# First batch loaded in four transfers on two queues, its second softmax placed later, second column pair whole, a new written order

## The chip, the cores and the metric

The kernel runs on one core of one Trainium2 chip. The metric is the device time of one execution in microseconds (us). The core has a matrix engine (PE, with a weight load PEld that runs beside it), a vector engine (DVE), a scalar engine (ACT), a general engine (POOL), and SyncE (SP), which here only issues transfers. Each engine runs its own instructions in the order in which they are written and waits for the others through semaphores. Transfers (DMAs) are issued by SP, ACT and POOL.

## The reference

Two stages. The first lets `x` [8, 8, 512, 64] (batch, head, row, feature) and `state` [8, 8, 32, 64] read each other by two softmaxes; the second is a two-layer network with a PReLU between, over the 544 rows of each batch, 4352 rows of 512 in all.

```python
a  = softmax(x @ state.T / 8)          # over the 32 states:  xread = a @ state   (512 rows)
a2 = softmax(state @ x.T / 8)          # over the 512 rows:   sread = a2 @ x      (32 rows)
rows = concat([xread, sread])          # heads side by side: 512 columns
h = rows @ w_in                        # 512 -> 2048
g = max(h, 0) + alpha * min(h, 0)      # alpha per column
out = g @ w_out                        # 2048 -> 512
```

All inputs and the output are float32.

## The kernel before

Everything is in float16 for PE, with sums in float32. The `xread` rows are never formed: per batch the kernel makes `m = state @ w_in` (step "m", its copy "mo"), and then `h = m.T @ a.T` directly. A batch has 16 column parts of 128 columns of `h` ("F", two 512-column matmuls each). Batch 0 can also be worked in pieces: "f" does a pair of column parts for one half of the rows (four 256-column matmuls), with "n" and "g" for its PReLU. The PReLU of a whole part is "N" on ACT (`neg = relu(-h)`) and "G" on DVE (`g = h + (1 - alpha) * neg`). The second layer of batch 0 is plain ("S" matmuls, "O" copies out). Batches 1 to 7, and a batch 8 which is the 256 `sread` rows, use seven products in place of eight ("P"), with sums of weights "W" and of activations "U" on POOL, kept copies "K" and quarters of the output "Q".

The attention steps of one batch are these. "lx" loads `x` (POOL's queue, cast to float16 on the way); "xd" transposes it by a DMA issued by SP into `xT`; for batch 0 PE transposes it ("xt", copies "xo"), since it is needed at once, and batch 1's is done likewise. "sc" are the scores. From them come two softmaxes:

- over the states: "sb" (a transpose on DVE), "smax", "ssh", "sexp" (ACT), "ssum", "snorm" and "wb" (a transpose on DVE), which gives `aT`, the moving operand of the column parts. For batch 0 the scores are computed a second time with the rows on the partitions ("tsc", from `st_pairs`, filled by "sbd"), in two halves, and `aT` comes by PE ("at", copies "ao").
- over the rows, for the state reads: "tm" (a maximum on DVE), "nb" (its scaling), "te" (two exponentials on ACT), "tsum", "tn", "tt" (a transpose by a DMA issued by SP into `e2T`), and then "rd" (32 small matmuls) with its copy "rdo" into `XS`. `XS` is wanted only by batch 8's column parts, near the end.

Before any of this "stc", "stt" and "sto" bring batch 0's states into `stT`, and "str" and "sro" the states of the other batches, in two groups (0: batches 1 and on, 1: the later ones), from the load "lst". "wi.0" to "wi.3" load `w_in` by 512 columns, "wo.0" to "wo.3" `w_out` by 512 rows, all on POOL's queue. "oma" makes `1 - alpha`.

What sets the order of the work is one string, `ORDER` (L18): a list of such steps, written out by hand, with their batch, part and PSUM bank or engine as arguments. The program runs through it and issues every step's instructions to the engines in that order; no scheduler moves them. `F.1.5.3` is batch 1, column part 5, PSUM bank 3; a letter behind a step is its engine (a: ACT, v: DVE, p: POOL). `Z.k.n` are n fill matmuls into bank k, whose result nobody reads; before the list starts there are 16 more of them. There are six single PSUM banks (k0 to k5) and one double ("two"), each with one buffer: a step that writes to a bank waits until the last reader of what stood there is done. So an early or late PReLU shows up as a wait of a matmul for its bank. Copies of the output go through four `osb` buffers (L643 and on, and L741 and on), each freed by the landing of the transfer that SP issues from it.

Ahead of the list stand, in this order: the load of batch 0's `x`, 512 KB per half `j` of the rows, both on SP (`load_x0`, L162); the load of batch 0's states on ACT's queue; a memset on DVE and four small loads of `alpha` on SP; the fill pattern and the identity on POOL; and the memset of `st_pairs` on DVE.

## Time and profile before

| | us |
|---|---|
| median of 3 runs | 213.96 (213.93 to 214.35) |
| the profiled execution | 214.07 |
| its span, first to last instruction | 212.0 |
| PE busy | 203.3 (96%), 2034 matmuls |
| DVE busy | 174.2 (82%) |
| ACT busy | 152.6 (72%) |
| POOL busy | 179.1 (84%) |
| granted TensorE clock, mean | 1.00 |

Times in the profile count from the first instruction of the span. Busy is the time in which an engine has work under way, also when that work stalls: matmuls are pipelined and their ends are modelled, so 96% says that PE is nearly always the engine at work, not that it runs at its peak. The chain of waits is followed back from the last instruction to whatever released each step. DVE's share is an average: near 100% over the middle of the span, and less towards the end, where no attention is left to do.

### The profile page before, as it was taken

Reading aid. Unit: us, or ns where it says so; the run is one execution under the profiler, and the core shown is the slowest. Engines: PE = TensorE matmul, PEld = TensorE weight load, DVE = VectorE, ACT = ScalarE, POOL = GpSimd, SP = SyncE. Lnnn points to the kernel's source line nnn. Section 1 sums busy time; section 2 is a strip of 40 time slices with the busy share of each in tenths; the row PEclk is TensorE's granted clock in tenths of the full one; section 3 lists DMA queues with packets and bytes.
Section 4 is the critical chain, followed back from the end, with each engine's and each line's share of the span. In section 5 each row is a group of like instructions: output and inputs, shape, how many; then the busy total and the mean of one; then the engine's idle time right before and its main releaser. Section 6 shows DMA issues by size and latency. Waiting matters only on the chain.

```text
span 212.0 us, 5108 instructions
## 1 busy us (share of the span) xinstructions
PE 203.3 (96%) x2034; PEld 137.7 (65%) x2034; DVE 174.2 (82%) x260; ACT 152.6 (72%) x300; POOL 179.1 (84%) x111
## 2 busy tenths in 40 slices
PE   7899999999999999999999998999999999999991
PEld 4556333444666665677667875667688777888880
DVE  0787988999999999999999999898999777654340
ACT  2577979999999999999797777887954584234100
POOL 8048848998999899999996999479996999999860
PEclk9999999999999999999999999999999999999999
DMA  6999995966665436778744539011521201111232
GB/s 159 219 204 207 206 204 89 160 165 90 152 105 89 106 84 135 110 134 143 183 117 49 103 106 192 3 51 40 162 53 49 99 3 49 49 53 49 74 124 102
DMA packets 43975, 23.70 MB, mean 112 GB/s; under 512 B 22192, under 2 KB 43440, under 8 KB 43952
## 3 DMA queue, kind: packets, MB, share of 16 engines
q1 hardware_dynamic: 31904, 15.22, 27.9%
q0 software_dynamic: 11776, 8.09, 26.6%
q8 instruction: 16, 0.26, 0.5%
q10 hardware_dynamic: 272, 0.07, 0.1%
q14 instruction: 7, 0.06, 0.1%
HBM read 17.31 MB, written 8.91 MB: 124 GB/s over the span
## 4 chain that ended last, share of the span: by engine, by line
PE 88%; DMA 7%; ACT 2%; issue 1%; SPq 0%; DVE 0%; ACTq 0%
PE h L556 25%; PE px L715 23%; PE pv L715 12%; PE o L626 6%; PE py L715 5%; PE m_ps L507 4%; PE h L565 3%; PE fill L236 3%; DMA xT<-xg 2%; DMA x<-in_x_dram 2%; PE sr_ps L480 2%; DMA out_dram<-oq 2%; DMA e2T<-e 1%; PE sc L314 1%; PE xT_ps L299 1%; PE h L578 1%
## 5 line engine op out<-in xcount | busy, mean ns | idle before, releaser
L612 DVE SCALAR_TENSOR_TENSOR g<-neg,oma_sb,h 128x512 f16<-128x512 f32 (+1 forms) x140 | 92.7, 708 | 11.6 <-ACT neg L609 11.1
L609 ACT ACTIVATE neg<-h 128x512 f32<-128x512 f32 (+1 forms) x140 | 75.0, 585 | 23.0 <-PE h L556 14.4
L556 PE MATMUL h<-aT,m 128*128 128x512 f16 x248 | 67.2, 379 | 0.1
L715 PEld LDWEIGHTS <-gsum 128*128 128x128 f16 x480 | 46.1, 98 | 16.8 <-issue 1.8
L715 PEld LDWEIGHTS <-g 128*128 128x128 f16 x360 | 35.0, 98 | 9.1 <-issue 0.9
L694 POOL TENSOR_TENSOR gsum<-g 128x1024 f16<-128x1024 f16 (+1 forms) x16 | 32.0, 2009 | 4.2 <-DVE g L612 3.6
L694 POOL TENSOR_TENSOR gsum<-g,g 128x1024 f16<-128x1024 f16 (+1 forms) x16 | 32.0, 2004 | 3.9 <-DVE g L612 3.8
L556 PEld LDWEIGHTS <-m 128*128 128x128 f16 x248 | 23.7, 98 | 15.5 <-issue 0.8
L694 POOL TENSOR_TENSOR gsum<-gsum,g 128x1024 f16<-128x1024 f16 (+1 forms) x16 | 32.1, 2006 | 1.1
L715 PE MATMUL px<-ws,gsum 128*128 128x256 f16 x240 | 32.6, 273 | 0.0
L694 POOL TENSOR_TENSOR gsum<-g,gsum 128x1024 f16<-128x1024 f16 (+1 forms) x16 | 31.9, 2005 | 0.1
L731 ACT COPY kept<-px 128x512 f32<-128x512 f32 (+1 forms) x22 | 12.7, 577 | 14.0 <-PE px L715 13.7
L533 ACT CAST m<-m_ps 128x512 f16<-128x512 f32 x36 | 20.0, 613 | 1.8 <-PE m_ps L507 1.5
L384 POOL TENSOR_TENSOR ts<-ts,mx 128x1024 f32<-128x1024 f32 x7 | 13.4, 1908 | 5.4 <-DVE mx L379 5.4
L715 PE MATMUL px<-w_out_sb,gsum 128*128 128x256 f16 x120 | 17.4, 273 | 0.0
L715 PE MATMUL pv<-ws,gsum 128*128 128x256 f16 x120 | 17.2, 273 | 0.0
L748 DVE TENSOR_TENSOR oq<-pv,kept 128x512 f32<-128x512 f32 (+1 forms) x16 | 10.5, 655 | 8.1 <-PE pv L715 6.7
L626 PE MATMUL o<-w_out_sb,g 128*128 128x512 f16 x64 | 17.1, 380 | 0.0
L715 PE MATMUL pv<-ws,g 128*128 128x256 f16 x120 | 16.9, 273 | 0.0
L715 PE MATMUL px<-w_out_sb,g 128*128 128x256 f16 x120 | 16.9, 273 | 0.0
L715 PE MATMUL py<-w_out_sb,g 128*128 128x256 f16 x120 | 16.2, 273 | 0.0
L531 ACT CAST m<-m_ps 128x1024 f16<-128x1024 f32 x12 | 12.4, 1032 | 1.3 <-PE m_ps L507 1.2
(76 smaller groups left out, 251.6 us busy)
## 6 DMA issues: line engine op xcount, KB each, us to landing
out_dram<-oq SPq DMA_DIRECT2D x28, 256.0 KB, 2.5
xg<-in_x_dram POOLq DMA_DIRECT2D x7, 512.0 KB, 6.9
w_in_sb<-in_moe_w_in_dram POOLq DMA_DIRECT2D x4, 512.0 KB, 9.3
...
```

The costliest lines, as they stand in the source:

```text
L384: engine(e).tensor_tensor(blocks(cols(live["ts", b], j, S)), blocks(scored(b, j)), over_blocks(cols(live["mx", b], j, S // N)), ALU.subtract,)
L507: nc.tensor.matmul(t[N * k : N * (k + 1), :], st_head(b, h)[64 * r : 64 * r + 64, :], w_in_sb[64 * r : 64 * r + 64, c, 512 * f : 512 * (f ...
L531: copier(e)(m_tile(b, f), t)
L533: copier(e)(m_tile(b, f)[:, g, :], t[g])
L556: nc.tensor.matmul(h.rearrange("p (r j s) -> p r j s", r=2, j=2), ms[b, f][:, g, 128 * j : 128 * (j + 1)], weights(b, g), start=(g == 0), ...
L609: nc.scalar.activation(neg, h, RELU, bias=0.0, scale=-1.0)
L612: nc.vector.scalar_tensor_tensor(g_tile(b, jc), negs.pop((b, jc)), oma_sb[:, jc : jc + 1], hs.pop((b, jc)), ALU.mult, ALU.add,)
L626: nc.tensor.matmul(outs[b, q], g_tile(b, jc)[:, 128 * q : 128 * (q + 1)], w_out_sb[:, jc, :], start=not begun and jc == 2 * jc2, stop=left ...
L694: engine(e).tensor_tensor(t, x(), y(), op)
L715: nc.tensor.matmul(pbanks[b, name][:, i, :], of(b, c)[:, j, 128 * i : 128 * (i + 1)], moving[:, 4 * c + j, :], start=not begun and j == 0, ...
L731: copier(e)(t, pbanks[b, "x"])
L748: nc.vector.tensor_tensor(osb, pbanks[b, name], kept[b, add], ALU.add)
```

## The change

It rewrites `ORDER` as a whole (1117 steps before, 1109 after; the same matmuls do the needed work, in another order) and edits the code around it:

- Batch 0's `x` comes in four loads of 256 KB (four heads each) in place of two of 512 KB. The first half of the rows is issued by SP, the second by ACT, behind the load of batch 0's states.
- `alpha`'s memset and loads become a step, "la", which stands behind the first loads of the weights; the two memsets go from DVE to POOL.
- The load of the other batches' states is split: "lst.0" stands behind "wi.0", "lst.1" far later, and "str.1" and "sro.1" with it.
- In the list, batch 0's second softmax (the scores "sc.0", then "tm.0", "nb.0", "te.0") stands behind batch 1's scores "sc.1" and the maxima and exponentials "te" made of them, in place of between the halves of the first softmax. Batch 1's scores come earlier.
- The second pair of column parts of batch 0 (parts 2 and 3) is done whole (`F.0.2`, `F.0.3`) in place of in two row halves (`f.0.1.0`, `f.0.1.1`).
- The casts of the second half of `x` are on ACT, that of batch 0's states on DVE.
- The loads of the weights go in another order: before `wi.0 lst lx.1 wi.1 wo.0 wo.1 wi.2 wi.3 wo.2 wo.3`, after `wi.0 lst.0 lx.1 wi.1 wi.2 wo.0 wo.1 wi.3 wo.2 wo.3`, with the two norms "snorm.p.0" between `wo.0` and `wo.1`.
- In batch 5, "tt.5" and "rd.5" stood next to each other but for one step "m"; now the column parts and products of batches 2 to 4 between them come to some 6 us of PE. At the end of the list the last copies out have new engines and places (`K.8.2` on ACT), and three fills stand last.
- The other steps have new places within their stage, and new banks. The fills of the list are 42 both before and after, in 16 groups before and 8 after.

The list's start and end, and the code:

```diff
-Z.0.3 stc.a stt.0 cx.0.1.v xt.0.0.1.1 xo.0.0.1.a wi.0 cx.0.0.v xt.0.0.0.2 xo.0.0.0.a sbd.0.v lst sbd.1.v Z.3.2 sto.a
-Z.3.2 Z.3.3 cx.1.0.v xt.0.1.0.3 cx.1.1.v tsc.0.1.4 tsc.0.0 smax.0.0 ssh.v.0.0 xo.0.1.0.a xt.0.1.1.5 xo.0.1.1.a Z.1.3
-Z.1.2 sc.0.0 sc.0.1 tsc.1.1.1 m.0.0.2.0 tsc.1.0 sexp.0.0 tm.0 smax.0.1 ssum.0.0 Z.3.3 mo.0.0.a.1 lx.1 Z.3.2 Z.3.2
-Z.3.3 ssh.v.0.1 str.1.3 nb.0.a te.0.1 Z.5.3 str.0.5 Z.4.3 Z.4.3 te.0.0 sexp.0.1 Z.4.2 mo.0.0.v.0 Z.4.3 wi.1 ssum.0.1
-wo.0 sro.0.a xt.1.0.0.4 snorm.p.0.0 at.0.0 ao.0.a wo.1 Z.1.3 tsum.0 snorm.p.0.1 xt.1.0.1.1 m.1.0 xt.1.1.0.2 sro.1.a
-wi.2 oma.a xo.1.0.0.v wi.3 xo.1.0.1.v xo.1.1.0.a f.0.0.0.5 xt.1.1.1.0 n.0.0.0 mo.1.0.v at.1.4 ao.1.v m.0.1.1.3
-tn.0.1.p mo.0.1.v.1 m.1.1 mo.1.1.a g.0.0.0.0 g.0.0.0.1 f.0.0.1.2 n.0.0.1 f.0.1.1.4 mo.0.1.a.0 n.0.1.1 f.0.1.0.3
-xo.1.1.1.v g.0.0.1.1 g.0.0.1.0 sc.1 tm.1 m.2.0.5.0 mo.2.0.a.1 mo.2.0.a.0 F.0.5.1 N.0.5 F.0.4.2 N.0.4 nb.1.a te.1.1
-g.0.1.1.0 g.0.1.1.1 G.0.5 S.0.3.0.0 wo.2 G.0.4 S.0.1.0.5 S.0.1.1 sb.1 F.0.7.4 N.0.7 G.0.7 F.0.6.1 wo.3 tn.0.0.p N.0.6
-S.0.3.1 G.0.6 n.0.1.0 g.0.1.0.0 S.0.2.2.2 S.0.3.2 te.1.0 S.0.1.2 S.0.2.0 g.0.1.0.1 m.0.2 S.0.2.3 S.0.1.3 smax.1
-mo.0.2.a F.0.8.4 N.0.8 G.0.8 W.1.1.p F.0.11.1 N.0.11 G.0.11 tsum.1 F.0.10.3 N.0.10 m.0.3 mo.0.3.a W.1.0.p lx.2 S.0.2.1
-S.0.3.3 F.0.9.4 m.1.2 F.0.12.1 ssh.p.1 sexp.1 G.0.10 S.0.2.5 S.0.1.5 ssum.1.s N.0.9 G.0.9 F.0.13.3 S.0.3.5 mo.1.2.a
-m.1.3 N.0.12 G.0.12 S.0.3.4 F.0.15.4 tn.1.1.a N.0.13 G.0.13 F.0.14.1 S.0.1.4 S.0.3.6 S.0.1.6 W.2.0.p S.0.2.4 N.0.15
...
-F.5.1.5 N.5.1 G.5.1 P.4.5.0.1 P.4.5.0.0 F.5.6.3 N.5.6 P.4.5.1.1 G.5.6 P.4.5.1.0 tt.5 m.7.1.1.2 rd.5.4 mo.7.1.a.0 sc.7
-rdo.5.a m.6.3.5.1 mo.6.3.a.0 U.4.3.0.p F.5.0.3 P.4.7.0.0.4 mo.7.1.a.1 tm.7 mo.6.3.a.1 F.5.13.5 P.4.7.1.0 N.5.13 N.5.0
...
-U.7.4.0.p N.8.0 G.8.0 F.8.10.5 U.8.3.1.p P.7.5.1.0 K.7.4.a P.8.2.0.1.2 N.8.10 G.8.10 P.7.7.1.0 P.8.1.0.0.4 U.8.3.0.p
-P.7.2.1.0.3 Q.7.1.1 P.7.2.0.1 P.7.2.0.0 P.7.3.0.1 P.7.2.1.1 U.8.1.0.p P.7.3.1.0 P.7.4.0.1 P.8.1.0.1 P.7.3.0.0 Q.7.0.0
-K.8.1.a P.7.4.1.1 U.8.2.0.p P.8.6.0.0 P.7.4.0.0 P.7.4.1.0 Q.7.1.0 U.8.1.1.p U.8.2.1.p P.8.6.0.1 K.8.2.v P.7.3.1.1
-P.8.7.0.0.5 P.8.5.0.1 P.8.5.0.0 K.8.4.a P.8.7.0.1 P.8.2.0.0 U.8.4.0.p Q.7.0.1.v P.8.3.0.0 Q.8.1.1 P.8.4.0.1 U.8.4.1.p
-P.8.4.0.0 Q.8.0.0 Q.8.1.0 P.8.3.0.1 Q.8.0.1.a
+cx.0.0.v xt.0.0.0.0 stc.v cx.0.1.v cx.1.0.a cx.1.1.a stt.1 xo.0.0.0.v xt.0.0.1.2 Z.3.3 sbd.0.v sbd.1.v tsc.0.0.3
+xo.0.0.1.v tsc.0.1 smax.0.0 xt.0.1.0.4 xo.0.1.0.v xt.0.1.1.5 sto.a wi.0 lst.0 xo.0.1.1.a Z.0.6 ssh.v.0.0 sexp.0.0 lx.1
+tsc.1.0.0 tsc.1.1 Z.2.6 smax.0.1 ssh.v.0.1 wi.1 ssum.0.0 m.0.0.2.1 mo.0.0.a.0 sexp.0.1 str.0.4 Z.5.9 ssum.0.1 Z.5.3
+sro.0.a wi.2 wo.0 m.1.0 mo.1.0.v la m.2.0.5.3 xt.1.1.0.0 xt.1.1.1.2 xo.1.1.1.v mo.0.0.a.1 xt.1.0.1.4 mo.2.0.a.0
+xo.1.1.0.a snorm.p.0.0 at.0.1 xo.1.0.1.a xt.1.0.0.5 xo.1.0.0.v ao.0.v snorm.p.0.1 at.1.0 ao.1.a Z.2.3 oma.a sc.1
+mo.2.0.a.1 f.0.0.1.2 sb.1 wo.1 F.0.2.4 n.0.0.1 N.0.2 m.0.1.5.1 wi.3 wo.2 Z.0.9 F.0.3.0 mo.0.1.a.1 mo.0.1.a.0 F.0.5.3
+tm.1 wo.3 g.0.0.1.1 smax.1 g.0.0.1.0 nb.1.a te.1.1 te.1.0 G.0.2 N.0.3 G.0.3 F.0.4.1 F.0.6.5 N.0.6 G.0.6 N.0.5 tsum.1
+G.0.5 m.0.2 mo.0.2.a f.0.0.0.2 F.0.7.4 N.0.7 G.0.7 N.0.4 G.0.4 S.0.1.0.0 n.0.0.0 ssh.p.1 lx.2 xd.2 S.0.1.1 g.0.0.0.0
+S.0.3.0.5 g.0.0.0.1 S.0.3.1 m.1.1 F.0.11.3 F.0.10.4 sexp.1 S.0.3.3 mo.1.1.a ssum.1.s W.1.0.p S.0.0.1.1 F.0.8.2 N.0.11
+S.0.1.3 G.0.11 N.0.10 G.0.10 N.0.8 G.0.8 S.0.3.2 S.0.0.0 m.0.3 mo.0.3.a F.0.9.3 N.0.9 S.0.0.3 S.0.1.2 sc.0.0 sc.0.1
+G.0.9 tm.0 F.0.12.4 N.0.12 F.0.13.2 F.0.14.3 G.0.12 N.0.13 S.0.3.5 nb.0.a te.0.0 W.1.1.p snorm.p.1 wb.1 G.0.13 W.2.0.p
+te.0.1 W.2.1.p S.0.1.4 tn.1.0.p S.0.0.5 F.0.15.4 N.0.15 G.0.15 tsum.0 N.0.14 G.0.14 S.0.1.5 m.1.3 S.0.3.4 F.1.2.2
+S.0.1.6 mo.1.3.a N.1.2 G.1.2 tn.0.1.p tn.1.1.p tn.0.0.p W.3.0.p F.1.7.4 N.1.7 G.1.7 F.1.5.3 N.1.5 S.0.1.7 O.0.1.a tt.0
+S.0.0.4 F.1.13.2 N.1.13 F.1.3.4 G.1.5 G.1.13 N.1.3 G.1.3 F.1.12.0 N.1.12 tt.1 G.1.12 F.1.14.3 N.1.14 G.1.14 m.1.2
+mo.1.2.a F.1.6.2 N.1.6 S.0.0.7 F.1.0.4 N.1.0 S.0.0.6 m.2.2.0.3 mo.2.2.a.1 mo.2.2.a.0 sc.2 G.1.6 lst.1 S.0.0.2 O.0.0.a
+tm.2 nb.2.a sb.2 smax.2 F.1.15.2 F.1.4.3 N.1.15 G.1.0 S.0.2.7.0 F.1.8.1 S.0.3.7 N.1.4 G.1.4 S.0.2.3 S.0.3.6 S.0.2.1
+W.3.1.p te.2.0 te.2.1 tsum.2 G.1.15 O.0.3.a F.1.1.4 N.1.1 N.1.8 m.3.2 rd.0.5 rdo.0.a rd.1.3 G.1.8 W.4.0.p str.1.2
+S.0.2.4 G.1.1 S.0.2.6 ssh.p.2 sexp.2 lx.3 S.0.2.2 S.0.2.5 rdo.1.a ssum.2.5 S.0.2.0 U.1.1.1.p mo.3.2.a sro.1.a
+U.1.3.0.p tn.2.1.p snorm.v.2 m.2.3.1.4 mo.2.3.a.0 m.2.1 O.0.2.v F.1.9.3 N.1.9 F.1.11.2 P.1.1.0.1.1 P.1.1.0.0 P.1.1.1.0
+N.1.11 mo.2.3.a.1 mo.2.1.a wb.2 F.1.10.5 G.1.9 F.2.8.0 F.2.11.4 N.1.10 U.1.2.1.p F.2.2.3 G.1.11 G.1.10 N.2.11 xd.3
...
+F.4.13.5 N.4.13 xd.6 P.2.3.1.0 Q.2.0.1.a U.3.1.1.p tn.5.0.a G.4.13 tn.5.1.a tt.5 U.3.2.1.p F.4.15.0 N.4.15 sb.5
+F.4.11.3 N.4.11 G.4.15 P.3.1.0.1.1 P.3.1.1.0 P.3.1.1.1 P.3.1.0.0 P.2.4.1.0 F.4.14.4 K.3.1.a Q.2.1.0 N.4.14 F.4.12.5
+F.4.1.0 P.3.6.1.0 G.4.11 N.4.1 G.4.14 G.4.1 P.3.6.0.0 N.4.12 G.4.12 F.4.10.2 N.4.10 G.4.10 sc.6 rd.5.3 rdo.5.a rd.4.4
...
+U.7.3.1.p K.8.1.a U.7.4.0.p U.7.4.1.p U.8.1.1.p P.7.7.0.1 P.7.7.1.1 P.7.3.0.1 P.7.3.1.1 Q.7.1.1 P.7.3.1.0 P.7.4.1.0
+P.7.4.1.1 P.7.4.0.1 U.8.1.0.p U.8.2.0.p P.7.4.0.0 Q.7.1.0 U.8.2.1.p P.8.6.0.1 P.8.6.0.0 K.8.2.a P.7.3.0.0 U.8.3.0.p
+P.8.7.0.0.5 Q.7.0.1.v P.8.5.0.1 P.8.5.0.0 K.8.4.a U.8.3.1.p P.8.7.0.1 P.8.2.0.1.4 U.8.4.0.p Q.8.1.1 U.8.4.1.p
+P.8.2.0.0 P.8.4.0.1 P.8.4.0.0 Q.8.0.0 Q.8.1.0 P.8.3.0.0 P.8.3.0.1 Q.8.0.1.a Z.1.3
...
 """
 
 
@@ -146,6 +145,8 @@
         return ps.tile(shape, dtype, name=name, tag="two", bufs=1)
 
     def copier(e):
+        if e == "p":
+            return nc.gpsimd.tensor_copy
         return nc.scalar.copy if e == "a" else nc.vector.tensor_copy
 
     def engine(e):
@@ -167,29 +168,35 @@
         xgs[0] = att.tile([128, H, 2, 2, D], F16, name="xg_0", tag="xg", bufs=3)
         for j in range(2):
             t = att.tile([128, H, 2, D], F32, name=f"x0_{j}", tag="ts", bufs=2)
-            nc.sync.dma_start(
-                t, x[0, :, 256 * j : 256 * (j + 1), :].rearrange("k (p r) d -> p k r d", r=2)
-            )
+            for g in range(2):
+                heads = slice(4 * g, 4 * g + 4)
+                (nc.scalar if j else nc.sync).dma_start(
+                    t[:, heads, :, :],
+                    x[0, heads, 256 * j : 256 * (j + 1), :].rearrange("k (p r) d -> p k r d", r=2),
+                )
             x0s.append(t)
 
     def x0_cast(j, g, e):
         copier(e)(xgs[0][:, 4 * g : 4 * g + 4, j, :, :], x0s[j][:, 4 * g : 4 * g + 4, :, :])
 
-    load_x0()
     rows = state.rearrange("b h n d -> (b h n) d")
     n0 = H * N
     n_j = (B * H * N - n0) // 128
     w_st = n_j // 2
     st0_32 = consts.tile([128, 2, D], F32)
     nc.scalar.dma_start(st0_32, rows[:n0, :].rearrange("(g p) d -> p g d", p=128))
+    load_x0()
     alpha_rows = consts.tile([128, N], F32)
-    nc.vector.memset(alpha_rows, 0.0)
-    for q in range(4):
-        nc.sync.dma_start(
-            alpha_rows[N * q : N * q + n_jc, :],
-            moe_alpha.rearrange("(jc q p) -> q jc p", q=4, p=N)[q],
-        )
     alpha_sb = consts.tile([128, N], F32)
+
+    def load_alpha():
+        nc.gpsimd.memset(alpha_rows, 0.0)
+        for q in range(4):
+            nc.sync.dma_start(
+                alpha_rows[N * q : N * q + n_jc, :],
+                moe_alpha.rearrange("(jc q p) -> q jc p", q=4, p=N)[q],
+            )
+
     pattern = consts.tile([128, 256], F16)
     nc.gpsimd.iota(
         pattern, pattern=[[37, 256]], base=-4800, channel_multiplier=29,
@@ -199,10 +206,10 @@
     make_identity(nc, ident)
     st = consts.tile([128, n_j, D], F16)
 
-    def load_states():
+    def load_states(i):
         nc.gpsimd.dma_start(
-            st.rearrange("p (i j) d -> p i j d", i=2),
-            rows[n0:, :].rearrange("(i p j) d -> p i j d", i=2, j=w_st),
+            st[:, w_st * i : w_st * (i + 1), :],
+            rows[n0:, :].rearrange("(i p j) d -> i p j d", i=2, j=w_st)[i],
         )
 
     w_in_sb = consts.tile([128, n_c, d_ff], F16)
@@ -227,7 +234,7 @@
     XS = consts.tile([128, n_c, 2, N, B // 2], F16)
 
     st_pairs = consts.tile([128, H, 2, N], F16)
-    nc.vector.memset(st_pairs, 0.0)
+    nc.gpsimd.memset(st_pairs, 0.0)
 
     def fill(k, n):
         t = single(k, f"fill_{len(zs)}", [128, 256], F32)
@@ -374,9 +381,9 @@
             return cols(live["ts", b], j, S)
         return live["tsc", j].rearrange("p r h n -> p (r h n)")
 
-    def state_max(b, j=None):
+    def state_max(b, j=None, e="v"):
         soft_tiles(b)
-        nc.vector.tensor_reduce(
+        engine(e).tensor_reduce(
             cols(live["mx", b], j, S // N), blocks(scored(b, j)), AX.X, ALU.max
         )
 
@@ -392,14 +399,14 @@
         ts = cols(live["ts", b], j, S)
         nc.scalar.activation(ts, ts, EXP, bias=0.0, scale=scale)
 
-    def state_sum(b, jk):
+    def state_sum(b, jk, e="v"):
         j = None if b else jk
         if jk == "s":
             live["r1", b] = att.tile([128, 2 * S // N], F32, name=f"r1_{b}", tag="r1", bufs=2)
         elif b:
             live["r1", b] = single(jk, f"r1_{b}", [128, 2 * S // N], F32)
         r1 = cols(live["r1", b], j, S // N)
-        nc.vector.tensor_reduce(r1, blocks(cols(live["ts", b], j, S)), AX.X, ALU.add)
+        engine(e).tensor_reduce(r1, blocks(cols(live["ts", b], j, S)), AX.X, ALU.add)
         nc.vector.reciprocal(r1, r1)
 
     def state_norm(e, b, j=None):
@@ -752,11 +759,11 @@
     steps = {
         "lst": load_states, "wi": load_w_in, "wo": load_w_out, "lx": load_x,
         "stc": first_states_cast, "stt": first_states_transposed, "sto": first_states_out,
-        "oma": one_less_alpha, "sbd": first_states_paired, "str": states_transposed, "sro": states_out,
+        "la": load_alpha, "oma": one_less_alpha, "sbd": first_states_paired, "str": states_transposed, "sro": states_out,
         "xd": x_transposed_dma, "xt": x_transposed, "xo": x_out, "sc": scores, "cx": x0_cast, "tsc": token_scores,
         "at": tokens_transposed, "ao": tokens_out,
         "sb": score_blocks, "smax": state_max, "ssh": state_shift, "sexp": state_exp,
-        "ssum": state_sum, "snorm": state_norm, "wb": weights_back,
+        "ssum": state_sum, "smx": lambda e, b: state_max(b, None, e), "ssm": lambda e, b: state_sum(b, "s", e), "snorm": state_norm, "wb": weights_back,
         "tm": token_max, "nb": token_shift, "te": token_exp, "tsum": token_sum, "tn": token_norm,
         "tt": token_transposed, "rd": state_reads, "rdo": state_reads_out,
         "m": state_w_in, "mo": state_w_in_out,
```

More of the change, by code (lines that the diff above doesn't have):

```diff
@@ new lines @@
+N.6.2 G.6.2 F.6.14.2 P.5.1.1.1.3 P.5.1.0.1 N.6.14 G.6.14 F.6.3.5 P.5.1.1.0 N.6.3 G.6.3 F.6.8.4 m.7.1.1.0 U.5.1.1.p
+rd.6.2 N.6.8 rdo.6.v mo.7.1.a.0 rd.7.5 U.5.1.0.p U.5.2.0.p rdo.7.a mo.7.1.a.1 F.6.15.1 F.6.6.2 N.6.6 P.5.2.0.0.5
+smax.7 P.5.1.0.0 U.5.2.1.p K.5.1.a F.6.11.0 N.6.11 N.6.15 G.6.8 G.6.6 G.6.11 G.6.15 F.6.4.4 F.6.1.2 P.5.6.0.0
+P.5.2.1.1 P.5.6.1.1 F.8.9.0 N.6.4 G.6.4 N.8.9 G.8.9 F.6.12.1 N.6.12 G.6.12 ssh.p.7 F.6.10.4 N.6.1 G.6.1 P.5.6.1.0
+P.5.6.0.1 K.5.2.a N.6.10 G.6.10 sexp.7 P.5.2.1.0 F.8.13.0 ssum.7.1 snorm.v.7 P.5.2.0.1 P.5.5.0.1 Q.5.0.0 U.5.3.1.p
```

107 lines of the change are left out of this document (47 added, 60 removed).

## The prediction

> **What bounds the kernel now.** I read the page's first part, then the groups by shape, then the chain, then the waits and the timeline of the first 40 us. The page (busy shares; the chain's shares):
>
> ```profile
> PE 203.3 (96%) x2034; PEld 137.7 (65%) x2034; DVE 174.2 (82%) x260; ACT 152.6 (72%) x300; POOL 179.1 (84%) x111
> ...
> PE 88%; DMA 7%; ACT 2%; issue 1%; SPq 0%; DVE 0%; ACTq 0%
> ```
>
> Groups of PE by shape (count; busy us, mean ns), then the chain that ended last (start, us, what) and PE's waits:
>
> ```profile
> L556 PE MATMUL h<-aT,m 128*128 128x512 f16 x248 | 67.2, 379 | 0.1
> ...
> L715 PEld LDWEIGHTS <-gsum 128*128 128x128 f16 x480 | 46.1, 98 | 16.8 <-issue 1.8 <-POOL gsum L694 0.4
> L715 PEld LDWEIGHTS <-g 128*128 128x128 f16 x360 | 35.0, 98 | 9.1 <-issue 0.9
> ...
> L626 PE MATMUL o<-w_out_sb,g 128*128 128x512 f16 x64 | 17.1, 380 | 0.0
> ...
> L236 PE MATMUL fill<-pattern 128*128 128x256 f16 x58 | 10.5, 306 | 1.8 <-POOL pattern L194 1.2
> ```
>
> ```profile
> 51.47 1.11 ACT neg L609 x2
> ...
> 62.55 1.31 PE px L715 x12
> 63.86 1.73 PE h L556 x8
> ...
> 129.30 2.85 DMA e2T<-e
> 132.29 0.68 PE sr_ps L480 x32
> ...
> 204.43 3.57 DMA out_dram<-oq
> 208.00 0.02 issue
> ...
> 208.18 0.37 ACT oq L746
> ```
>
> ```profile
> PE sr_ps L480 <- DMA e2T<-e: 1.0, 1, 1.0
> PE xT_ps L299 <- DVE xg L176: 0.5, 1, 0.5
> PE sc L314 <- DMA xT<-xg: 0.4, 1, 0.4
> ```
>
> The chain is PE. Back to back, a 256-column matmul takes 1.31/12 = 0.109 us and a 512-column one 1.73/8 = 0.216 us. So the needed stream is 840 x 0.109 + (248 + 64) x 0.216 = 159 us, and some 30 us of smaller groups (m, transposes, scores, reads, batch 8): 188.7 us, the same before and after. The span is this, plus what PE loses, plus the end. I count loss as start of an instruction minus the needed work ordered ahead of it. The 58 fills are loss too. Where it arises is read from the timeline of the start:
>
> ```profile
> 7.18 0.76 DVE L176 CAST xg<-x 128x512 f16<-128x512 f32 x2 [0.36 <-DMA x<-in_x_dram]
> ...
> 9.41 0.69 DVE L384 TENSOR_TENSOR ts<-tsc,mx 128x512 f32<-128x512 f32 x1
> ...
> 10.09 1.23 DVE L426 TENSOR_REDUCE nb<-sc 128x2 f32<-128x1024 f32 x1
> ...
> 10.14 0.63 ACT L393 ACTIVATE ts<-ts 128x512 f32<-128x512 f32 x1 [0.61 <-DVE ts L384]
> ...
> 11.59 0.69 ACT L443 ACTIVATE e<-sc,nb 128x512 f16<-128x512 f32 x1
> ...
> 12.26 0.68 ACT L443 ACTIVATE e<-sc,nb 128x512 f16<-128x512 f32 x1
> ...
> 14.03 0.69 DVE L402 TENSOR_REDUCE r<-ts 128x16 f32<-128x512 f32 x1
> ...
> 14.75 0.25 DVE L403 RECIPROCAL r<-r 128x16 f32<-128x16 f32 x1
> ...
> 15.16 1.04 POOL L406 TENSOR_TENSOR an<-ts,r 128x512 f16<-128x512 f32 x1 [0.41 <-ACT stT L282]
> ...
> 17.36 0.91 ACT L282 COPY stT<-st_ps 128x896 f16<-128x896 f16 x1
> ...
> 18.12 0.60 PE L578 MATMUL h<-aT,m 128*128 128x256 f16 x4
> ...
> 18.32 0.58 ACT L304 COPY xT<-xT_ps 128x512 f16<-128x512 f16 x1
> ...
> 22.09 4.22 POOL L670 TENSOR_TENSOR ws<-w_out_sb 128x1024 f16<-128x1024 f16 x2 [1.44 <-DMA w_out_sb<-in_moe_w_out_dram]
> ...
> 24.04 1.40 DVE L612 SCALAR_TENSOR_TENSOR g<-neg,oma_sb,h 128x512 f16<-128x512 f32 x2
> ...
> 38.23 0.59 PE L556 MATMUL h<-aT,m 128*128 128x512 f16 x2
> ```
>
> Ahead of the first column part (18.12) stand 4.2 us of needed work: 13.9 lost. Ahead of batch 1's first column (38.23) stand 22.6: 15.6 lost. So nearly all loss is the start. Later come 3.0 us: about 1.0 to 1.1 in the read of batch 5's e2T at 132.29, about 0.5 in batch 3's scores, 1.3 in small steps between m matmuls and other banks. PE ends at 207.5, but the last copy starts at 208.18, behind an output's landing (204.43 + 3.57): it reuses that output's buffer.
>
> **The change, part by part.**
>
> First x. The same 1 MB and the 64 KB of states move, in four loads on two queues instead of two on one. Today the second half of x lets its cast start at 7.18. No row shows x on ACT's queue. Bounds: the rate of today with the last part 1 us later (8.2), or the second half as early as the first half is now, whose cast starts 7.18 - 0.36 less the 0.88 us of casts, 5.9 at the most. I take 7.0, nearest to today's row. The casts of that half move to ACT (0.57 each, by the 0.58 of its copies).
>
> The Trainium skill, "DMA: Bandwidth & Descriptors", section "Issuing engines are not separate DMA queues", says that loads issued from several engines run on the same 16 DMA engines, and that only issue time is saved. By that rule the landing stays near 7.2 and the sum loses 0.2 us.
>
> Batch 0's softmax. Today DVE's maximum for the reads (1.23 at 10.09) and ACT's two exponentials (0.67 apart) sit between the two halves of the other softmax. They, the scores and the nb step go behind. What follows, by rows: last cast done 7.6; transposes and copy to 8.7; second scores 9.4; maximum 0.69 to 10.1; shift 0.69 to 10.8; m.0.0 and its copy go ahead on ACT (0.5), exponential 0.63 to 11.9; sum and reciprocal 0.69 + 0.25 to 12.9; POOL's norm 1.04 to 14.05. Today that norm ends at 16.2. Then ACT is the bound: state copy (to 12.7), two m copies, two xT copies, aT copy, each 0.5 apart, to 16.0. Scores of batch 1 go at 16.0, the first part at 16.4 with 4.5 us of work ahead: 11.9 lost against 13.9.
>
> The gain is partly given back. Batch 1's softmax now comes before batch 0's columns: transpose, two maxima (some 1.2 each, as the row at 10.09) on DVE, two exponentials on ACT, while PE runs nine fills of Z.0.9 (1.4 us with the change of bank) and then waits for the scores' bank (exponential done 20.75, m.0.2 at 20.9) and for G.0.3 (22.25). From there each G takes 1.40 - 0.74 = 0.66 us from start to start and each N 1.11 - 0.61 = 0.50, and I place them one by one behind their matmuls and banks: S.0.1.0 at 22.4 with 8.5 us ahead (13.9 lost), F.0.8 at 26.2 with 12.3 (13.9), F.0.15 at 32.7 with 18.6 (14.1), F.1.5 at 35.8 with 21.5 (14.3). Today 15.6. **Start: -1.3 us**, -0.3 to -2.0.
>
> Loads on POOL's queue. They land one behind the other; issue to landing:
>
> ```profile
> L212 POOL DMA_DIRECT2D w_in_sb<-in_moe_w_in_dram x4: 747/792/972, 1.6 to 17.0; - x4
> ...
> DMA to landing us min/median/max: 7.8/9.3/12.7
> ```
>
> The third part of w_in now stands ahead of the first of w_out, and half the states go later (lst.1). First w_out: POOL's row at 22.09 shows the second one landing at 22.1, and a load takes some 2.5 us, so the first lands at 19.5 today; 2.5 later, less 0.6 for the states and 0.2, it lands at 21.2, and its first use is at 22.4. The others have 1 to 3 us of cover. If that cover is gone, each us late is a us lost. lst.1 issues at about 39 and is read by PE at about 48: free. The alpha loads move behind the w_in loads, are used at 15.8, and are free; POOL's two memsets (0.1 and 0.3 us) fall into its idle start.
>
> Second column pair whole. Eight 256-column matmuls become four of 512: PE the same. DVE saves 4 x 0.48 - 2 x 0.74 = 0.4 us, off the path.
>
> Places anew. tt.5 stood right ahead of rd.5 with one m step between; now some 6 us of PE work stand between: **-1.1 us**, -1.1 to 0. The wait of batch 3's scores: lx.3 goes behind ssh.p.2 on POOL, xd.3 can issue at about 55 and land at 59.6, the scores come at 60.7. I put it at 0 (-0.5 to +1). The end: the last output's buffer is freed one product earlier relative to PE's end (ten products follow Q.7.0.1's last one, nine before), and a copy ahead of it moves from DVE to ACT: **-0.5 us** of the 0.65 between 207.5 and 208.18, at most -0.65. The three fills at the very end run beside the output.
>
> Against it stands DVE, busy all through the middle:
>
> ```profile
> 60.00:110.00 50.00, 50.00 (x514) 33.35 (x513) 48.58 (x70) 47.14 (x94) 48.40 (x27) 1.00 0.65 128
> ```
>
> (columns: PE, PEld, DVE, ACT, POOL busy.) Ahead of batch 4's last G stand 103.8 us of PE work today and 101.0 after, with 1.5 us more DVE work: 4.3 us less cover. DVE gained 2.2 us at the start, PE 1.3. By this DVE runs up to 3.4 us behind the place where its step is written, against 2.8 today. The next user of that bank (m.6.2) then waits about 0.9, and some 0.2 falls elsewhere: **+1.1 us**, 0 to +4.
>
> **Sum** against the profiled execution (214.07: span 212.0 and 2.07 around it, 0.1 above the median of 213.96): -1.3 - 1.1 + 0 - 0.5 + 1.1 = -1.8, so 212.3.
>
> **The rivals.**
>
> (a) DVE keeps up. Its term is 0: 211.2. For it: 1.4 of 50 us is idle today.
>
> (b) The gains only fill DVE's lag. PE arrives early and waits in batches 3 to 5 until DVE has come to the same point, and the term is 2.8 us: 214.0, no change. For it: 48.58 of 50.
>
> (c) Slower: DVE's places are too tight at wb.4, G.4.4 and wb.6 (3.1 to 3.4 us behind) because the PSUM banks cover only about 1 us there. The waits add to some 4 us, 215.2. It decides from 3.0 us on. Against it: today's 2.8 us were borne without a wait.
>
> (d) The x loads on ACT's queue start late (8.2): +1.1, 213.4. For it: the states on that queue land at 4.7, though they have an eighth of the bytes of x's first half.
>
> (e) The clock. In the start the order leaves PE some 40% busy from 4.4 to 8. If the clock fell there, about 1 us of matmuls on the path would take twice as long for a while: +0.5, 212.8. The profile's row above has the granted clock at 1.00, and so has every stretch from 0 on, through gaps of 0.7 us.
>
> The Trainium skill, "TensorE: Matmul & The Clock Gate", section "HAM oscillation — how this bites in real kernels", asks for no idle gap over about 3.4 us; the longest in my chain is 0.8, so that rule gives (e) little.
>
> **How the numbers follow.** Forecast (211.7 to 213.2) 0.37; (a) 0.13; (b) 0.14; (c) 0.26; (d) 0.07; (e) 0.03. The predicted time is the forecast's, 212.3. The range 210.8 to 215.2 takes in the bounds of (a) with the best start and (c)'s centre; it leaves out about 0.2. About 0.2% (0.4 us) is what a measurement of this kernel can tell. Faster: forecast, (a), (e) and most of (d), 0.58; same: (b) and a little of (d), 0.16; slower: (c), 0.26.
>
> **What would show it.** Right: the second half of x cast on ACT near 7; POOL's second norm ending near 14; first part of batch 0 near 16.4; F.1.5 near 35.8; no PE wait for e2T of batch 5; last ACT copy right at PE's end. Wrong: a PE loss of over 15.6 us at F.1.5, w_out landing after 22.4, or gaps of PE in 90 to 130 us that end with DVE.

## The result, and the profile after

The changed kernel takes 212.08 us in the median (210.96 to 214.54, 4 runs) against 213.95 (213.93 to 214.35, 4 runs): a ratio of 0.9891, with a 95% interval of 0.9851 to 0.9931. The forecast was 212.3, and faster. The profiled execution took 212.13 us, its span is 210.0; before, 214.07 and 212.0. So between the two profiled executions the difference is -1.9. The ratios leave out runs more than 1.5% above the fastest of the same kernel (here the one of 214.54, whose mean granted clock was 0.992); the medians count all.

The kernel before repeats to 0.4 us here, and to 0.7 to 1.1 in the sets of runs below. The changed one does not: even its runs with a mean granted clock of 0.999 or more, here and in the next set, lie between 209.6 and 212.1. Much of what follows is about that spread.

The page of the changed kernel (busy; the chain's shares):

```profile
PE 201.0 (96%) x2030; PEld 137.0 (65%) x2030; DVE 172.8 (82%) x255; ACT 152.5 (73%) x301; POOL 180.0 (86%) x114
...
PE 79%; DVE 7%; DMA 7%; ACT 4%; issue 1%; ACTq 1%
```

The totals hardly differ, as the needed work is the same. PE's waits, and four pieces of the chain that ended last (start, us, what):

```profile
PE xT_ps L306 <- ACT xg L180: 2.1, 1, 2.1
PE fill L243 <- POOL pattern L201: 1.2, 1, 1.2
PE sc L321 <- DMA xT<-xg: 0.9, 1, 0.9
PE h L563 <- DVE g L619: 0.5, 1, 0.5
PE xT_ps L306 <- DVE xg L180: 0.2, 1, 0.2
```

```profile
1.85 7.17 DMA x<-in_x_dram
9.04 0.63 ACT xg L180
...
56.12 6.79 DMA xT<-xg
```

Before, PE waited 1.0 for batch 5's `e2T` and 0.4 for batch 3's `xT`. The first wait is gone; the second has become 0.9; a wait of 0.5 for DVE is new; and the last quarter of `x`, on ACT's queue, lands 7.17 us after its issue, at 9.0. The timeline:

```profile
1.25 1.15 ACTq L173 DMA_DIRECT2D x<-in_x_dram  x2
...
2.11 0.97 POOL L219 DMA_DIRECT2D w_in_sb<-in_moe_w_in_dram  x1
...
9.71 0.40 PE L306 MATMUL xT_ps<-ident,xg 128*128 128x128 f16 x4 [2.14 <-ACT xg L180]
...
13.70 2.06 POOL L413 TENSOR_TENSOR an<-ts,r 128x512 f16<-128x512 f32 x2 [6.79 <-DVE r L410]
...
17.25 0.61 PE L585 MATMUL h<-aT,m 128*128 128x256 f16 x4
...
46.95 0.59 PE L563 MATMUL h<-aT,m 128*128 128x512 f16 x2 [0.49 <-DVE g L619]
...
62.95 0.41 PE L321 MATMUL sc<-xT,stT 64*32 64x256 f16 x16 [0.93 <-DMA xT<-xg]
...
206.35 0.37 ACT L753 COPY oq<-px 128x256 f32<-128x256 f32 x1 [2.63 <-PE px L722]
```

With the prediction's count (start minus the needed work ordered ahead) PE has lost 15.06 us at F.1.5.3, which starts at 36.52 behind 21.47 of work. Before it was 15.6 at the like place. At batch 3's scores it is 17.2, against 16.4 before: here the changed kernel is behind, and the little that the start had won is gone. From there to the end it loses 0.3 more, the kernel before 2.2, among them 1.1 in the read of batch 5. The last copy stands right behind PE, where it had waited 0.65 for a buffer. So in this execution the gain arises behind batch 3's scores, and not in the start.

### The profile page after: what moved, and what is told of

The parts are those of the page before. It is cut to its first block, busy times and chain, and to the rows that moved or that the text cites. A ratio compares the mean times of both kernels' runs of the same rounds, so it can differ in the third digit from the quotient of the medians.

```text
span 210.0 us, 5107 instructions
## 1 busy us (share of the span) xinstructions
PE 201.0 (96%) x2030; PEld 137.0 (65%) x2030; DVE 172.8 (82%) x255; ACT 152.5 (73%) x301; POOL 180.0 (86%) x114
## 4 chain that ended last, share of the span: by engine, by line
PE 79%; DVE 7%; DMA 7%; ACT 4%; issue 1%; ACTq 1%
PE px L722 25%; PE h L563 21%; PE pv L722 13%; PE py L722 5%; DMA x<-in_x_dram 3%; PE m_ps L514 3%; PE h L572 3%; DMA xT<-xg 3%; PE o L633 3%; DVE g L619 3%; PE sr_ps L487 2%; ACT neg L616 2%; DVE nb L433 2%; PE fill L243 2%; DVE ts L353 1%
## 5 line engine op out<-in xcount | busy, mean ns | idle before, releaser
L619 DVE SCALAR_TENSOR_TENSOR g<-neg,oma_sb,h 128x512 f16<-128x512 f32 (+1 forms) x142 | 94.1, 709 | 11.4 <-ACT neg L616 11.3
L616 ACT ACTIVATE neg<-h 128x512 f32<-128x512 f32 (+1 forms) x142 | 76.4, 585 | 24.6 <-PE h L563 12.8
L722 PEld LDWEIGHTS <-gsum 128*128 128x128 f16 x480 | 46.6, 98 | 13.8 <-issue 1.4
L563 PEld LDWEIGHTS <-m 128*128 128x128 f16 x252 | 24.1, 98 | 17.2 <-issue 2.1
L540 ACT CAST m<-m_ps 128x512 f16<-128x512 f32 x37 | 20.9, 604 | 3.6 <-PE m_ps L514 3.6
L722 PE MATMUL py<-w_out_sb,g 128*128 128x256 f16 x120 | 17.2, 273 | 0.0
L722 PE MATMUL pv<-ws,gsum 128*128 128x256 f16 x120 | 16.4, 273 | 0.0
L722 PE MATMUL px<-w_out_sb,gsum 128*128 128x256 f16 x120 | 16.4, 273 | 0.0
L633 PE MATMUL o<-w_out_sb,g 128*128 128x512 f16 x64 | 16.3, 379 | 0.0
L722 PE MATMUL pv<-ws,g 128*128 128x256 f16 x120 | 15.9, 273 | 0.0
```

What stands on the lines that cost most here:

```text
L540: copier(e)(m_tile(b, f)[:, g, :], t[g])
L563: nc.tensor.matmul(h.rearrange("p (r j s) -> p r j s", r=2, j=2), ms[b, f][:, g, 128 * j : 128 * (j + 1)], weights(b, g), start=(g == 0), ...
L616: nc.scalar.activation(neg, h, RELU, bias=0.0, scale=-1.0)
L619: nc.vector.scalar_tensor_tensor(g_tile(b, jc), negs.pop((b, jc)), oma_sb[:, jc : jc + 1], hs.pop((b, jc)), ALU.mult, ALU.add,)
L633: nc.tensor.matmul(outs[b, q], g_tile(b, jc)[:, 128 * q : 128 * (q + 1)], w_out_sb[:, jc, :], start=not begun and jc == 2 * jc2, stop=left ...
L722: nc.tensor.matmul(pbanks[b, name][:, i, :], of(b, c)[:, j, 128 * i : 128 * (i + 1)], moving[:, 4 * c + j, :], start=not begun and j == 0, ...
```

## The experiments

Three sets, each with its own runs of the kernel before on the same chip: 214.2, 214.5 and 214.4 in the median.

**The changed kernel again.** No edit.

> The changed kernel once more, unchanged, to see its spread and a second trace. In its first trace the last quarter of x (second load on ACT's queue) lands at 9.01 us and batch 3's scores wait 0.9 us for xT; its runs went from 210.96 to 212.13. Theory A (the spread comes from the landing of that quarter, against the loads of the weights): times differ by as much as the landing does, so a run near 211.0 has the quarter landing near 7.5 to 8. Theory B (the spread is the wait of batch 3's scores for xT): the landing stays at 9.0 +- 0.2 and the wait is near 0 in a run near 211.0. Theory C (neither): both as in the first trace, 212.1.

210.96 in the median of six, ratio 0.984 (0.9808 to 0.9873). The four with a mean clock of 1.000 lie from 209.6 to 211.53; 211.99 and 213.02 had 0.992 and 0.984. Its profiled execution took 210.40, 1.73 less than the first. From its chain and its waits of PE:

```profile
1.85 6.15 DMA x<-in_x_dram
```

```profile
PE fill L243 <- POOL pattern L201: 1.2, 1, 1.2
PE xT_ps L306 <- ACT xg L180: 0.8, 1, 0.8
PE h L563 <- DVE g L619: 0.5, 1, 0.5
```

The quarter landed at 8.0 instead of 9.0 and the wait for `xT` is absent. The loss at F.1.5.3 is 14.05, 1.0 less; at batch 3's scores it is 15.1, 2.1 less. A is right about the landing and B about the wait: two landings move from run to run.

**All four quarters on SP.**

```diff
-                (nc.scalar if j else nc.sync).dma_start(
+                nc.sync.dma_start(
```

> The changed kernel with all four quarters of x issued by SP. Theory A (ACT's queue shares with POOL's loads and is what makes the last quarter late): the last quarter lands at 7.2 as in the kernel before, first column part of batch 0 at about 16.2 instead of 17.25, PE loss at S.0.1.0 near 13.9 instead of 14.5, and the time falls by 0.5 to 1.0 us, to some 211.2. Rival (the start is bound by ACT's copies and the state loads, not by the last quarter): the landing moves, the time doesn't: 212.1 +- 0.3. Second rival (one queue is slower as a whole): last quarter at 8 or later, the first ones later too, 212.5.

216.63, ratio 1.011 (1.0092 to 1.0129): slower than before. The fourth quarter is issued at 2.40, behind the first part of `w_in`, and lands at 10.7; the chain and the windows of the start (columns: PE, PEld, DVE, ACT, POOL busy, granted clock, DMA share, GB/s):

```profile
2.40 8.26 DMA x<-in_x_dram
```

```profile
8.00:9.00 1.00, 0.40 (x4) 0.23 (x4) 0.49 (x2) 0.18 (x1) 0.00 (x0) 1.00 1.18 202
9.00:10.00 1.00, 0.00 (x0) 0.00 (x0) 0.69 (x2) 0.00 (x0) 0.00 (x0) 0.83 1.33 202
10.00:11.00 1.00, 0.00 (x0) 0.00 (x0) 0.00 (x0) 0.32 (x1) 0.00 (x0) 0.50 1.45 196
...
15.00:16.00 1.00, 0.94 (x15) 0.44 (x16) 0.96 (x3) 0.12 (x1) 0.00 (x0) 0.50 1.23 204
16.00:17.00 1.00, 1.00 (x18) 0.85 (x15) 0.21 (x1) 1.00 (x3) 0.63 (x1) 0.76 1.25 209
```

PE waits 2.7 us, the clock is at a half from 9.7 to 16.5, and the loss at S.0.1.0 is 18.3 instead of 14.5. The profiled execution took 220.59, since the clock fell a second time (67.7 to 74.5, around another wait of 2.7 for batch 3's `xT`); the other five lie from 216.0 to 216.9, with mean clocks of 0.976 to 0.984. Theory A is refuted: it isn't ACT's queue that makes the quarter late. What this run has in common with the first trace is that the last quarter is issued at about the time of, or behind, `w_in`'s first part.

**The load of batch 4's `x` later.**

```diff
-mo.3.3.a.1 lx.4 smax.3 m.5.0.5.0 U.1.1.0.p U.1.2.0.p U.1.4.0.p
+mo.3.3.a.1 smax.3 m.5.0.5.0 U.1.1.0.p U.1.2.0.p U.1.4.0.p lx.4
```

> The changed kernel with the load of batch 4's x (lx.4) three POOL steps later, behind the transfer that transposes batch 3's x. Theory A (the two transfers run at the same time, and this is the 0.9 us wait of batch 3's scores): xd.3 takes 4.3 to 4.8 us from issue to landing instead of 6.8, the wait goes, PE's loss at the end falls from 17.4 to 16.4, 211.2. Rival B (DVE has no slack in batches 3 to 5, as the prediction's term says): the wait goes, but PE waits for DVE instead, 211.8 to 212.1. Rival C (the transfer is late for another reason): xd.3 still takes over 6 us, 212.1.

211.56, 209.81 to 212.51, ratio 0.9862 (0.9825 to 0.9899), beside 210.96 for the unchanged one: no gain that can be told. Its profiled execution (209.81) has no wait for `xT`, but the second trace of the unchanged kernel had none either. Its `x` quarter landed at 7.4, 5.55 us after its issue by its chain, and its loss at F.1.5.3 is 13.45. Over the three executions the landing goes 9.0, 8.0, 7.4 and that loss 15.06, 14.05, 13.45: in these three the start follows the landing us for us.

The transposing transfer of batch 3 took 4.3 us, as A has it. But in the second trace of the unchanged kernel it took 4.3 too, with batch 4's load issued 2.1 us behind it. In the first trace it was itself issued late (at 56.1 instead of 53.6), because the load of batch 3's `x` had taken 7.3 us instead of 5.8; batch 4's load then followed within 0.6 us.

**The kernel before with the four loads alone.** `load_x0` as in the change, the list as before.

> The kernel before with only x changed: four loads, two on SP, two on ACT behind the states. Theory A (in the kernel before, whose both casts of the second half are on DVE in one row, the last quarter is late by 1.9 us too): last quarter near 9.0, second scores and everything behind them late, PE loss at the first column part 14.9 to 15.8 instead of 13.9, 214.5 to 215.8: the four loads alone cost time. Rival (they help, as the first quarters land at 4.2 instead of 5.4): 213.0 to 213.9.

214.5 against 214.2, 213.37 to 215.41 over 12 runs, ratio 1.0015 (0.9997 to 1.0032). In its chain the last quarter lands at 9.0 again, 7.17 us after its issue, and the loss at the first column part is 14.96, 1.04 more than before. Theory A: alone, the four loads gain nothing and bring the spread.

**The changed kernel with two loads of 512 KB on SP.**

```diff
-            for g in range(2):
-                heads = slice(4 * g, 4 * g + 4)
-                (nc.scalar if j else nc.sync).dma_start(
...
+            nc.sync.dma_start(
+                t, x[0, :, 256 * j : 256 * (j + 1), :].rearrange("k (p r) d -> p k r d", r=2)
+            )
```

> The changed kernel with x in two loads of 512 KB on SP again (the states' load still first on ACT, the casts and the order as changed). Theory A (what counts is whether the last piece of x is issued before POOL issues the first part of w_in at 2.1 us: two issues are through at 1.8): the last half lands at 7.2 in every run, as in the kernel before; first column part of batch 0 near 15.7; about 210.2, and the runs lie within 0.8 of each other instead of 2.4. Rival (four loads are quicker by themselves, and their spread is something else): first half at 5.4 in place of 4.2 and 5.3 makes the start later, 211.5 to 212.5, with the same spread.

211.56, ratio 0.9865 (0.9844 to 0.9887). The second half is through at 7.3, as A has it:

```profile
6.33 0.40 PE L306 MATMUL xT_ps<-ident,xg 128*128 128x128 f16 x4 [1.65 <-DVE xg L180]
...
7.33 1.14 ACT L180 CAST xg<-x 128x512 f16<-128x512 f32 x2 [4.79 <-DMA x<-in_x_dram]
```

```profile
8.00:9.00 1.00, 0.96 (x13) 0.81 (x14) 0.51 (x2) 0.73 (x2) 0.00 (x0) 0.50 1.25 202
9.00:10.00 1.00, 1.00 (x9) 0.84 (x8) 1.00 (x3) 0.36 (x1) 0.00 (x0) 0.50 1.40 194
10.00:11.00 1.00, 0.94 (x7) 0.50 (x5) 0.41 (x1) 0.78 (x2) 0.00 (x0) 0.50 1.49 199
```

But the first half comes 1.4 later than a quarter does (5.62 against 4.26 for its cast), PE stands still for 1.65 us, and in this execution the clock is at a half for 3.4 us. A was right on the landing, 1.4 too low in time, and wrong on the spread: four of the five runs lie from 211.01 to 212.37, the fifth took 214.87. The rival named 211.5 to 212.5. That small first pieces are worth having fits this, but no run shows it apart from the clock.

**The states' first group ahead of `w_in` on POOL's queue.**

```diff
-sto.a wi.0 lst.0 xo.0.1.1.a
+sto.a lst.0 wi.0 xo.0.1.1.a
```

> The changed kernel with the load of the states' first group ahead of the first part of w_in on POOL's queue, so that w_in's first part is issued at some 2.7 instead of 2.1 us, and x's last quarter (issued on ACT's queue from 1.85 to 2.41) stands ahead of it. Theory A (order of issue against w_in): the last quarter lands at 7.5 or earlier each time, spread under 0.8, about 210.0; w_in's first part lands some 0.5 later, near 10.0, with m.0.0 wanted at 10.3. Rival (the two queues share at random, whatever was issued first): landing between 7.4 and 9.0 and a spread of 2 us as before, median 211 to 212.

209.68, ratio 0.9806 (0.9767 to 0.9844), the fastest of all. Four of six runs lie from 209.27 to 209.74. The quarter is cast at 7.50, and `w_in` is issued at 2.87:

```profile
2.87 0.78 POOL L219 DMA_DIRECT2D w_in_sb<-in_moe_w_in_dram  x1
...
7.50 0.62 ACT L180 CAST xg<-x 128x512 f16<-128x512 f32 x1 [1.06 <-DMA x<-in_x_dram]
```

The profiled execution was the slowest of the six, 212.36. Batch 3's transposing transfer takes 7.09 us in its chain, and

```profile
PE sc L321 <- DMA xT<-xg: 1.7, 1, 1.7
```

That is one part. The other is in the start: the first column part begins at 16.75, 9.25 us behind the quarter's cast, where it is 8.2 in the three traces with landings of 9.0, 8.0 and 7.4. Six fills show it, first here, then in the first trace of the changed kernel:

```profile
8.97 1.28 PE L243 MATMUL fill<-pattern 128*128 128x256 f16 x6
```

```profile
9.94 0.82 PE L243 MATMUL fill<-pattern 128*128 128x256 f16 x6
```

Here PE still steps at half speed until about 9.9 us (0.213 us from one fill to the next instead of 0.109). So A holds for the landing (order of issue against `w_in`), but not for the spread, which is 3.1 us over the six: batch 3's `xT` still moves, and so does the time at which PE comes to full speed.

**The kernel before with batch 5's transposed read earlier.**

```diff
-K.4.1.a tn.5.0.a wb.5
+K.4.1.a tn.5.0.a tn.5.1.a tt.5 wb.5
...
-U.4.2.1.p tn.5.1.p Q.4.0.0
+U.4.2.1.p Q.4.0.0
...
-P.4.5.1.0 tt.5 m.7.1.1.2
+P.4.5.1.0 m.7.1.1.2
```

> The kernel before with the second norm of batch 5 on ACT right behind the first, and the transfer that transposes its e2T (tt.5) right behind that, some 8 us earlier. Theory A (the prediction's term: the read of batch 5 waited 1.1 us only because its transfer was issued late): no wait of PE at rd.5, PE loss at the end 17.5 instead of 18.6, 213.1 against 214.2. Rival B (ACT, which takes 0.7 more there, or DVE passes the wait on): a new wait elsewhere, 213.8 to 214.2.

214.21 against 214.51, ratio 0.9994 (0.9976 to 1.0012). The wait at rd.5 is gone, but the scores of batch 7, two steps behind, now wait 0.6 for their own transfer (batch 3's wait 0.7 in this execution, ahead of the edit):

```profile
PE sc L314 <- DMA xT<-xg: 1.2, 2, 0.7
```

Rival B: alone, the 1.1 us are not to be had in the kernel before. In the changed kernel the whole neighbourhood had moved, and neither wait is there.

**The kernel before with a free buffer at the end.**

```diff
-name=f"oq_{b}_{th}_{dh}", tag="osb", bufs=4)
+name=f"oq_{b}_{th}_{dh}", tag="osb" if b < B else "neg", bufs=4)
```

> The kernel before with the four outputs of batch 8 in buffers of the negatives, which are free by then, instead of the output buffers that they wait for. Theory A (the prediction's term of the end: the last ACT copy waits 0.65 us for a buffer): last copy right behind PE's last matmul, 213.6 against 214.2. Rival B (another output's transfer, or the queue, ends last all the same): 214.1 to 214.2.

213.63 against 214.51, ratio 0.9964 (0.9951 to 0.9977). The last copy no longer waits for a transfer, and Theory A has the time:

```profile
207.50 0.37 ACT L746 COPY oq<-px 128x256 f32<-128x256 f32 x1 [2.30 <-PE px L715]
```

**Both repairs on the changed kernel**: the states first and batch 4's `x` later.

> The changed kernel with both repairs: the states' first group ahead of w_in's first part on POOL's queue, and batch 4's x loaded behind the transfer of batch 3's. Theory A (the two are the whole spread of the changed kernel: one moved x's last quarter by up to 1.6 us, the other the scores of batch 3 by 0 or 1.2 to 1.9): last quarter near 7.5, no wait of batch 3's scores, 209.3 to 209.8 in nearly every run. Rival (another transfer is late by chance): runs over 210.5 remain though both are repaired.

211.07, 210.68 to 213.1, ratio 0.9877 (0.9839 to 0.9915): no better than the first repair alone (which ran on another chip), and no run under 210.5. The start is the best of all (loss at F.1.5.3 13.29; in the five traces with the first repair the quarter lands from 7.2 to 7.8) and batch 3's scores don't wait. But batch 4's `x` now travels with the transposed read of batch 2, what follows it on the queues is late, and the read of batch 3 waits:

```profile
PE sr_ps L487 <- DMA e2T<-e: 0.8, 1, 0.8
```

In this trace the second repair only moves the wait: the rival held. It is not there each time: of the five traces with batch 4's `x` later, three have it (0.8, 1.3, 1.0) and two don't.

**1.2 us more DVE work in batch 4's column parts**, on the last kernel.

```diff
-m.6.3.0.5 smax.5 rdo.4.a
+m.6.3.0.5 smax.5 smax.5 rdo.4.a
```

> The kernel with both repairs and the maximum over the states of batch 5 taken twice (the same result again): 1.2 us more DVE work among batch 4's column parts, where the prediction put DVE 3.4 us behind and PE waiting 0.9. Theory A (DVE has slack there; the trace of the changed kernel has it at most 2.4 us behind and no wait of PE): at most +0.3. Rival B (DVE is at its limit, as the prediction had it): +0.9 to +1.2.

Medians 211.18 and 211.07, a difference of 0.1. The profiled execution, in which the clock fell for a while as well (below), shows PE waiting once more for DVE behind the added step:

```profile
113.56 0.59 PE L563 MATMUL h<-aT,m 128*128 128x512 f16 x2 [0.32 <-DVE g L619]
```

So DVE takes in most of a further 1.2 us: Theory A, by the medians.

**Without the nine fills of Z.0.9**, on the kernel with both repairs.

> The kernel with both repairs without the nine fills of Z.0.9, behind which batch 0's column part 3 stands. Theory A (the prediction's working: what follows waits for the scores' bank and for m.0.1's copy anyway, so the fills cost nothing): within 0.2 of the kernel with both repairs. Rival B (they stand in PE's way): -0.4 to -1.2. Rival C (they keep the clock up, and without them it falls): +0.3 and more, with a granted clock below 1.00 behind 18 us.

210.81 against 211.07, 209.82 to 211.39. From batch 1's scores to S.0.1.0 the loss grows by 1.65 without the fills and by 1.64 with them; PE waits 0.8 for the copy of `m` instead. The medians differ by 0.26, a little more than Theory A's 0.2, but each lies inside the other's runs. By the loss the fills are free, and behind 18 us the clock stayed at 1.00: Theory A.

**Batch 0's softmax for its state reads back between the halves of the first**, on the kernel with both repairs.

```diff
-tsc.1.0.0 tsc.1.1 Z.2.6 smax.0.1
+sc.0.0 sc.0.1 tsc.1.0.0 tsc.1.1 Z.2.6 tm.0 smax.0.1
...
-mo.0.0.a.0 sexp.0.1
+mo.0.0.a.0 nb.0.a te.0.1 te.0.0 sexp.0.1
...
-S.0.1.2 sc.0.0 sc.0.1 G.0.9 tm.0 F.0.12.4
+S.0.1.2 G.0.9 F.0.12.4
...
-S.0.3.5 nb.0.a te.0.0 W.1.1.p
+S.0.3.5 W.1.1.p
...
-te.0.1 W.2.1.p
+W.2.1.p
```

> The kernel with both repairs, and batch 0's softmax for its state reads (scores, maximum, scaling, two exponentials) back between the halves of the first one, as in the kernel before. Theory A (it stood in the way of the start, 1.2 us on DVE and 1.6 on ACT between the halves): PE loss at S.0.1.0 greater by 1.0 to 1.8, time +1.0 to +1.8, to 210.5 to 211.4. Rival B (ACT's copies or the loads bound the start, and the room that DVE and ACT win behind 30 us gives it back): +0.3 or less.

212.84 against 211.07 (two of its nine runs took 216; without them 212.73), ratio to before 0.993 (0.9905 to 0.9954). The loss at S.0.1.0 is 14.11 against 12.73, at F.1.5.3 14.91 against 13.29. In the start DVE's maximum and ACT's exponentials stand where the prediction had them, and PE waits for ACT's copy of the states:

```profile
9.53 1.22 DVE L433 TENSOR_REDUCE nb<-sc 128x2 f32<-128x1024 f32 x1 [0.34 <-PE sc L321]
...
14.45 0.63 PE L514 MATMUL m_ps<-w_in_sb,stT 64*32 64x512 f16 x16 [1.42 <-ACT stT L289]
```

Theory A in the difference (its 210.5 to 211.4 had started from a lower time): moving this softmax is worth 1.4 to 1.8 us in the kernel with both repairs, about half of the 3.3 us by which that kernel is faster than the one before. How much of it the changed kernel without repairs gets, no run shows apart.

## Why the prediction was right, and which of its terms were not

The direction was right, and the mechanism named first, the start, is borne out by the runs that changed it. That the time came out within 0.2 us of 212.3 is luck. In the first trace the start brought 0.55 of its 1.3 us, and PE lost 1.35 more than before on the way to batch 3's scores. The read of batch 5 (-1.1), small waits behind those scores (-0.8, in the sum at nothing) and the end (-0.65) then made the time, to within 0.2 us; and DVE's +1.1 never came. The next six runs of the same kernel gained 3.2 us in the median, where the forecast had 1.7.

Three of the named signs were missed in that trace by 0.9 to 2 us: the cast on ACT at 9.0 (7), POOL's second norm ending at 15.8 (14), the first part at 17.25 (16.4). F.1.5 at 36.5 (35.8) was nearer; the read without a wait and the last copy at PE's end came as said.

- **Start, -1.3.** First trace -0.55 (15.06 against 15.6), second -1.55, with both repairs -2.3. The term that was mis-sized is the landing of the second half of `x`, put at 7.0 with bounds of 5.9 and 8.2: it was 9.0, 8.0 and 7.4. The upper bound came from the rate of the kernel before; it missed that the order of issue against `w_in` matters. The rest of the chain, from 7.6 to the first part at 16.4, was too long: with a landing at 7.4 the first part starts at 15.65, with 9.0 at 17.25. The two errors have opposite signs, so in the first trace the places after it came out within 0.7: S.0.1.0 at 23.0 (22.4), F.0.8 at 26.9 (26.2), F.1.5 at 36.5 (35.8).
- **Rival (d), x late on ACT's queue.** The event came, at a higher price than given (9.0, not 8.2), but the queue wasn't the cause, as the run with all four quarters on SP shows. The Trainium skill, "DMA: Bandwidth & Descriptors", section "Issuing engines are not separate DMA queues", says that loads from several engines run on the same 16 DMA engines. The trace agrees: from 7 to 8 us 208 GB/s moved, before and after. It says that the issue time saved is usually small beside the transfer; here a small shift in issue mattered all the same: with `w_in` issued 0.8 us later, the landing went from 7.4 to 9.0 down to 7.2 to 7.8.
- **Batch 0's softmax.** Confirmed by putting it back, in the kernel with both repairs: +1.4 in loss at S.0.1.0. The fills at 18.6 cost nothing, as the working had it.
- **e2T of batch 5, -1.1.** The wait is gone in every trace of the changed kernel. But the prediction did not ask what is late next: in the kernel before it was the scores of batch 7, and there the move alone brought nothing that can be told (0.3 in the medians, 0.1 by the ratio).
- **xT of batch 3, 0 (-0.5 to +1).** +0.5 in the first trace, -0.4 in the second, +1.3 in one repaired run. `xd.3` was put at 55 to 59.6 and ran from 56.1 to 62.9, with batch 4's load (lx.4) issued 0.6 us behind it. The prediction hadn't looked at that load. Where batch 3's own load was through in 5.8 us instead of 7.3 (second trace), `xd.3` ran from 53.6 to 57.9 and the scores didn't wait.
- **DVE, +1.1 in batches 3 to 5.** There PE doesn't wait for DVE in either trace of the changed kernel, and another 1.2 us of DVE work, in the kernel with both repairs, costs about 0.1. The cover that was counted as lost wasn't needed. A wait of 0.5 stands at 46.95 instead, in batch 1, where batch 2's maximum and transposes come between two G steps; the sum had nothing there. Rivals (a), (b) and (c) all turned on this term, and (a)'s mechanism is what happened, though not at (a)'s time.
- **The end, -0.5.** 0.65 of wait is gone; a free buffer alone in the kernel before brought 0.9 (0.5 to 1.05 by the interval).
- **Small waits.** Those between m matmuls and banks, taken as unchanged, fell from some 1.1 to 0.3 behind batch 3's scores. No run was made on them.
- **Rival (e), the clock.** In the first trace it held through 2.1 us of standstill at 7.6 to 9.7. In three of the kernel's own ten runs the mean was 0.984 to 0.992, and in the traces of three experiments it fell for a while. The chance of 0.03 was low. It leant on the clock's column, which reads 1.00 from 0 on; but in the kernel before, too, the fills ahead of 4 us step 0.213 us and later ones 0.109, so that column says nothing about the first microseconds.

What isn't settled: why the landing of a quarter whose issue on ACT (1.85 to 2.40) overlaps that of `w_in` on POOL (2.11 on) varies between 7.4 and 9.0; whether the order of the two issues counts or the 0.8 us between them; what holds up the load of batch 3's `x` (5.8 us in one run, 7.3 in another); when PE comes to full speed; and which of the new places took away the small waits.
